# Two more ScalarE functions (ln, exp) in place of a VectorE add and reciprocal, in the sigmoid of a small condition vector

## The chip, the cores and the metric

The kernel runs on one core of one Trainium2 chip. The metric is device time in microseconds (us), from runs of the whole program. Before the change the median was 267.67 us of three runs (267.42 to 267.75). Times inside a run are from its one profile, in us from the start of the span.

## The reference, cut to what matters

The program is one transformer block with an adaptive layer norm. A condition vector `c` of 512 numbers is turned into six vectors that scale, shift and gate the rest:

```python
mod = (_silu(c) @ w_mod).reshape(c.shape[0], 6, 1, -1)
sa, ca, ga, sb, cb, gb = (mod[:, 0].copy(), mod[:, 1].copy(), ...)   # cut
h = _layernorm(x, axis=-1) * (1 + ca) + sa
x = x + ga * _A_ref(h, A_wqkv, A_wo)        # attention, window of 256
h = _layernorm(x, axis=-1) * (1 + cb) + sb
x = x + gb * _B_ref(h, B_w1, B_b1, B_w2, B_b2)   # MLP over the tokens
```

`x` is 2048 x 512, `w_mod` 512 x 3072. `silu(c) = c * sigmoid(c)` is 512 numbers, and all that follows needs it.

## The kernel before

The condition lies as a tile `c4` of 4 partitions by 128. Its sigmoid is exp on ScalarE, then add and reciprocal on VectorE. TensorE transposes silu (`st`), and two groups of 16 small matmuls (`fm`, tile `ps_fm`) multiply it with two slices of `w_mod`, which give the shift `sa` and the scale `ca`. Further names in the profiles: `mv` is the mean and variance of a tile of x, `nm` and `rs` are made from it (minus the mean, one over the root of the variance), `xn` is the normalised x, `sT` the copy of the transposed silu, `pxy` also the target of the warm-up matmuls, `lz` and `et` are the logarithm and the exponentials of the attention.

```python
o1 = op("em", {"ACT": 0.23}, lambda e: ac.activation(out=em[:], in_=c4[:], func=ACT.Exp, scale=-1.0), deps=[o_c4], pos=-20)
o2 = op("em1", {"DVE": 0.13}, lambda e: ve.tensor_scalar_add(out=em[:], in0=em[:], scalar1=1.0), deps=[o1], pos=-20)
o3 = op("rm", {"DVE": 0.9}, lambda e: ve.reciprocal(out=rm[:], in_=em[:]), deps=[o2], pos=-20)
o4 = op("silu", {"DVE": 0.2}, lambda e: ve.tensor_tensor(out=silu4[:], in0=c4[:], in1=rm[:], op=ALU.mult), deps=[o3], pos=-20)
o5 = op("st", {"PE": 0.03}, e_stps, deps=[o4], pos=-20, cls="D", alloc="psd")
```

Two further parts matter. First, TensorE starts with warm-up matmuls on a tile of zeros, whose result nobody reads; there are 24, and 14 of them stand in front of `st` in TensorE's order:

```python
warm_ops = [op("warm", {"PE": 0.213}, e_warm, pos=-30.0 + n * 0.3, cls="D") for n in range(WARM)]
```

Second, the order of instructions on every engine is fixed by a list of numbers (`ORDER`), so the program keeps a later instruction of an engine behind one that waits. On VectorE the add and the reciprocal stand between the statistics of the first and the second tile of x, and silu stands behind the latter. The table of functions for exp and ln is loaded once, at the start: `nc.scalar.preload_act_table_set("natural_log_exp_and_others")`.

The softmax here doesn't subtract the row's maximum and nothing guards it: scores larger than these inputs give would overflow.

## Time and profile before

| What | Before |
|---|---|
| span of the profiled run | 265.2 us |
| TensorE, VectorE, ScalarE busy | 248.8, 195.5, 185.4 us |
| the add and the reciprocal on VectorE | 0.21 and 0.94 us |
| silu ready | 6.58 us |
| last of the 14 warm-ups starts | 6.61 us |
| transposition `st` starts | 6.92 us |
| second slice of `w_mod` landed | 7.24 us |
| both groups of `ps_fm` ended | 8.41 us |
| first large exponential of the attention (`et`) starts | 17.73 us |

### The profile page before, as it was taken

What the parts mean: (1) busy time and instruction counts of PE and PEld (TensorE: products, weight loads), DVE (VectorE), ACT (ScalarE), POOL (GpSimd) and SP (SyncE); (2) the same over time, 40 slices, a digit from 0 to 9 for tenths busy, and PEclk for the clock granted to TensorE, in tenths of its full rate; (3) what the DMA queues carried; (4) which work ended last, traced back from release to release, by engine and by line L of the source; (5) the groups of instructions that cost most, each with busy time, mean ns of one, the idle gap of its engine ahead of it and who ended that gap; (6) DMA issues with size and microseconds to landing.
All of it is one profiled execution on the core that took longest, in us unless ns stands there. A gap on an engine that the chain in (4) does not pass through costs nothing.

```text
span 265.2 us, 10676 instructions
## 1 busy us (share of the span) xinstructions
PE 248.8 (94%) x4769; PEld 136.8 (52%) x4769; DVE 195.5 (74%) x444; ACT 185.4 (70%) x268; POOL 91.1 (34%) x153
## 2 busy tenths in 40 slices
PE   7898999999989888899999999999999999999993
PEld 2575666656656654455544454445444444444441
DVE  7768896777847559999948888999998730415875
ACT  2479999999999899999999999999416432000000
POOL 8054321495289946543893031440000000000000
PEclk9999999999999999999999999999999999999999
DMA  6996400000018000000015872011499800001122
GB/s 205 362 381 206 47 5 4 5 2 5 2 31 213 5 4 5 0 5 2 4 27 136 220 184 79 5 44 40 143 373 397 355 4 0 20 0 63 59 99 79
DMA packets 31598, 25.34 MB, mean 96 GB/s; under 512 B 6076, under 2 KB 29632, under 8 KB 31552
## 3 DMA queue, kind: packets, MB, share of 16 engines
q1 hardware_dynamic: 31544, 24.66, 29.5%
q8 instruction: 37, 0.61, 0.9%
q14 instruction: 9, 0.07, 0.1%
q10 hardware_dynamic: 8, 0.00, 0.0%
HBM read 22.55 MB, written 2.10 MB: 93 GB/s over the span
## 4 chain that ended last, share of the span: by engine, by line
PE 67%; ACT 19%; DVE 8%; issue 4%; POOL 0%; ACTq 0%; POOLq 0%
PE pu L194 32%; ACT et L194 16%; PE pxy L194 13%; PE psa L194 8%; PE pq L194 5%; PE pa L194 4%; PE pv L194 3%; ACT lz L194 3%; DVE st L194 2%; DVE VT L194 1%; PE pt L194 1%; DVE part L194 1%; PE psb L194 1%; DVE h L194 1%; DVE mv L194 0%
## 5 line engine op out<-in xcount | busy, mean ns | idle before, releaser
L194 ACT ACTIVATE et<-psa 128x1536 bf16<-128x1536 f32 x75 | 109.2, 1455 | 4.0 <-PE psa L194 1.9
L194 PE MATMUL pu<-hb,w1p 128*128 128x512 bf16 x224 | 53.2, 380 | 0.7 <-DVE part L194 0.7
L194 PE MATMUL pu<-guT,w 128*128 128x512 bf16 x224 | 49.0, 379 | 0.0
L194 ACT ACTIVATE et<-psb 128x512 bf16<-128x512 f32 x75 | 45.1, 601 | 0.0
L194 PE MATMUL pxy<-et,ones_bd 128*32 128x192 bf16 (+3 forms) x960 | 38.7, 233 | 0.7 <-issue 0.7
L194 PE MATMUL pxy<-et,VT 128*32 128x192 bf16 (+3 forms) x960 | 38.4, 234 | 0.9 <-DVE OT L194 0.5
L194 PEld LDWEIGHTS <-w 128*128 128x128 bf16 x224 | 21.9, 98 | 26.4
L194 PE MATMUL psa<-QT,KT 32*128 32x192 bf16 (+3 forms) x720 | 30.0, 230 | 5.6 <-ACT et L194 4.9
L194 POOL TENSOR_SCALAR KT<-kb,mask_par 128x512 bf16<-128x512 bf16 (+1 forms) x36 | 22.9, 645 | 31.0 <-DVE kb L194 22.3
L194 PEld LDWEIGHTS <-w1p 128*128 128x128 bf16 x224 | 20.2, 98 | 25.6 <-issue 2.3
L194 PE MATMUL pq<-h1T,wqkv 128*128 128x512 bf16 (+1 forms) x128 | 30.1, 355 | 0.3 <-ACT VT L194 0.3
L194 PEld LDWEIGHTS <-KT 32*128 32x128 bf16 x960 | 16.2, 92 | 26.4 <-issue 24.1
L194 PEld LDWEIGHTS <-VT 128*32 128x32 bf16 x960 | 23.6, 96 | 11.6 <-issue 10.1
L194 PE MATMUL psb<-QT,KT 32*128 32x192 bf16 (+3 forms) x240 | 29.4, 231 | 0.0
L194 DVE SCALAR_TENSOR_TENSOR o<-pu,b2FM,bc_all 128x512 f32<-128x512 f32 x16 | 11.6, 748 | 20.2 <-PE pu L194 20.1
L194 DVE TENSOR_TENSOR et<-et,maskt 128x512 bf16<-128x512 bf16 (+2 forms) x56 | 24.9, 480 | 0.6 <-ACT et L194 0.5
L194 PEld LDWEIGHTS <-ones_bd 128*32 128x32 bf16 x960 | 23.2, 97 | 1.0 <-issue 0.9
L194 DVE BATCH_NORM_STATS2 st<-x 128x6 f32<-128x512 bf16 x32 | 21.8, 680 | 0.2
L194 DVE TENSOR_TENSOR OT<-pxy,lz 128x256 bf16<-128x256 f32 x32 | 13.4, 419 | 10.6 <-ACT lz L194 10.1
L194 PEld LDWEIGHTS <-wqkv 128*128 128x128 bf16 x192 | 14.0, 97 | 13.4 <-issue 4.8
L194 PE MATMUL pv<-wqkv,h1T 128*32 128x256 bf16 x512 | 17.9, 274 | 0.2 <-DVE VT L194 0.2
L194 PE MATMUL pa<-wod,OT 128*128 128x512 bf16 x64 | 17.3, 381 | 0.3 <-ACT part L194 0.3
(113 smaller groups left out, 355.1 us busy)
## 6 DMA issues: line engine op xcount, KB each, us to landing
w1p<-in_B_w_dram SPq DMA_DIRECT2D x14, 512.0 KB, 6.3
w<-in_B_w_dram SPq DMA_DIRECT2D x14, 512.0 KB, 8.3
wmod<-in_w_mod_dram SPq DMA_DIRECT2D x6, 512.0 KB, 5.5
x<-in_A_x_dram SPq DMA_DIRECT2D x16, 128.0 KB, 4.6
out_dram<-otile SPq DMA_DIRECT2D x16, 128.0 KB, 1.7
wqkv<-in_A_wqkv_dram SPq DMA_DIRECT2D x2, 384.0 KB, 5.5
wqkv<-in_A_wqkv_dram SPq DMA_DIRECT2D x1, 512.0 KB, 5.3
wod<-in_A_wo_dram SPq DMA_DIRECT2D x1, 512.0 KB, 8.7
```

The costliest lines, as they stand in the source:

```text
L194: ins = call(*args, **kwargs)
```

## The change

The intent is to take the slow reciprocal off VectorE: 1/(1+y) is computed as exp(-ln(1+y)), all on ScalarE, which idles there.

```diff
-    o2 = op("em1", {"DVE": 0.13}, lambda e: ve.tensor_scalar_add(out=em[:], in0=em[:], scalar1=1.0), deps=[o1], pos=-20)
-    o3 = op("rm", {"DVE": 0.9}, lambda e: ve.reciprocal(out=rm[:], in_=em[:]), deps=[o2], pos=-20)
+    o2 = op("em1", {"ACT": 0.25}, lambda e: ac.activation(out=rm[:], in_=em[:], func=ACT.Ln, bias=1.0), deps=[o1], pos=-20)
+    o3 = op("rm", {"ACT": 0.25}, lambda e: ac.activation(out=rm[:], in_=rm[:], func=ACT.Exp, scale=-1.0), deps=[o2], pos=-20)
```

In the built program VectorE has two instructions fewer and ScalarE two more. TensorE, GpSimd and the DMA queue have the same instructions in the same order.

## The prediction

> **What bounds the kernel now.** I read the page first, for which engine carries the span, then the chain that ended last in order of time over the first 30 us, because the changed operations run once, near the start. The first line below is the busy time of the engines, the second the share of the chain by engine.
>
> ```profile
> PE 248.8 (94%) x4769; PEld 136.8 (52%) x4769; DVE 195.5 (74%) x444; ACT 185.4 (70%) x268; POOL 91.1 (34%) x153
> ...
> PE 67%; ACT 19%; DVE 8%; issue 4%; POOL 0%; ACTq 0%; POOLq 0%
> ```
>
> TensorE is busy nearly throughout and carries two thirds of the chain. VectorE is busy for 74% of the span but carries 8% of the chain, so a microsecond of VectorE is by default not a microsecond of kernel. The question is whether this particular microsecond is one of the 8%. The chain around it (start, duration, what):
>
> ```profile
> 1.33 5.66 PE pxy L194 x14
> 6.99 0.10 PE st_ps L194
> 7.09 0.54 PE pxy L194 x2
> 7.63 0.78 PE ps_fm L194 x32
> 8.41 0.47 PE psb L194 x8
> ```
>
> The reader is to see that from 1.33 us to 6.99 us the chain lies on fourteen matmuls into pxy. They are the warm-up matmuls on a zeroed tile, whose results nobody reads. Right behind them comes st_ps, the transposition of silu(c), which is the only consumer of what the change touches. No link of the sigmoid (em, rm, silu) is in the chain. Next the timeline of VectorE alone from 4.2 us to the end of its row of work (start, duration, operation):
>
> ```profile
> 4.36 0.18 DVE L194 BATCH_NORM_AGGREGATE mv<-st 128x2 f32<-128x6 f32 x1
> 4.46 0.21 DVE L194 TENSOR_SCALAR em<-em 4x128 f32<-4x128 f32 x1
> 4.70 0.94 DVE L194 RECIPROCAL rm<-em 4x128 f32<-4x128 f32 x1
> 5.57 0.62 DVE L194 BATCH_NORM_STATS2 st<-x 128x6 f32<-128x512 bf16 x1
> 6.23 0.18 DVE L194 BATCH_NORM_AGGREGATE mv<-st 128x2 f32<-128x6 f32 x1
> 6.33 0.25 DVE L194 TENSOR_TENSOR silu<-c,rm 4x128 bf16<-4x128 bf16 x1
> 6.51 0.14 DVE L194 SCALAR_TENSOR_TENSOR nm<-mv 128x2 f32<-128x2 f32 x1
> ```
>
> VectorE has no idle time here: the statistics of the second x tile wait behind the reciprocal, silu waits behind those, and silu is ready at 6.33 + 0.25 = 6.58 us. ScalarE in the same stretch:
>
> ```profile
> 0.79 1.28 ACT L204 ACT_TABLE_LOAD   x1 [0.79 <-PEq L1251]
> 2.17 0.31 ACT L194 ACTIVATE em<-c 4x128 f32<-4x128 bf16 x1
> 6.45 0.30 ACT L194 ACTIVATE rs<-mv,eps_t 128x2 f32<-128x2 f32 x1 [3.97 <-DVE mv L194]
> 6.78 0.20 ACT L194 ACTIVATE rs<-rs 128x2 f32<-128x2 f32 x1
> ```
>
> It idles 3.97 us between em and rs, which is exactly where the two new functions go. Last, the handover itself, from the timeline of all engines:
>
> ```profile
> 6.92 0.09 PEld L194 LDWEIGHTS <-silu 4*128 4x128 bf16 x1 [0.42 <-DVE nm L194]
> 6.92 0.17 PE L194 MATMUL st_ps<-identity,silu 4*128 4x4 bf16 x1
> ...
> 7.13 0.16 DVE L194 COPY sT<-st_ps 128x4 bf16<-128x4 bf16 x1 [0.48 <-PE st_ps L194]
> ```
>
> The bracket says that the weight load of silu sat 0.42 us and was released by VectorE. So the deadline is nearly a tie: silu is ready at 6.58 us, and TensorE comes to it at about 6.8 us. I take that number from the last warm-up matmul, which I saw start at 6.61 us; at the fast cadence of 0.22 us it hands over at 6.83 us. The transposition started at 6.92 us, about 0.09 us later than that.
>
> **What the Trainium skill says.** "ScalarE: Activation LUTs", section "What ACT_TABLE_LOAD costs", gives an ACTIVATE with immediate scale and bias 186 ns + 0.833 N, and about 93 ns more for a pointer operand. For N = 128 that is 293 ns; the trace has 0.31 us for em. The pointer term agrees too: rs with the eps_t bias takes 0.30 us, rs without it 0.20 us, on the same shape. The same page, section "Table sets: the hidden batching unit", says that natural_log_exp_and_others holds both exp and ln. The kernel loads that set at its start (the one load of 1.28 us above) and already runs ln and exp for rs back to back with no load between 6.45 and 6.98 us, so the trace agrees. "TensorE: Matmul & The Clock Gate", Part 1, says that the first matmuls run with a start-to-start of 426.7 ns at N = 512 and later ones at 215.7 ns, and that the moment of the change depends on a free-running window and so varies between runs. Here the warm-ups step at about 0.43 us from the first on and only the last step, 6.39 to 6.61 us, is 0.22 us, so the cadences agree; that the moment varies is not shown by one trace.
>
> **The change part by part.** *Removed from VectorE:* the add (0.21 us) and the reciprocal (0.94 us). What counts is not their sum but how far the row behind them can move up: the second statistics start at 5.57 us and could start where the add started, 4.46 us, which is 1.11 us. Nothing else holds them, as the second x tile was issued at 1.2 us and landed 2.1 us later, about 3.35 us. So mv is done at about 5.30 us, silu at 5.47 us and nm at 5.54 us. The order of VectorE's other instructions is unchanged in the built program, as are all of TensorE's, GpSimd's and the DMA queue's.
>
> *Added to ScalarE:* ln of 4x128 with a bias: 0.31 (row em) plus at most 0.09-0.10 (rs with a bias against rs without) = 0.40 us; exp of 4x128: 0.31 us. With two handovers of 0.03 us (rs to rs: 6.75 to 6.78 us), rm is ready at 2.48 + 0.03 + 0.40 + 0.03 + 0.31 = 3.25 us. Silu cannot run before about 5.2 us because the statistics stand in front of it, so ScalarE has almost 2 us in hand. The 0.71 us of new ScalarE work costs nothing: it lies in the idle 3.97 us. rs follows mv at about 5.3 us.
>
> *Moved:* silu 6.58 to 5.47 us. Its consumer cannot start before the fourteen warm-ups are through, about 6.83 us, so of the 1.11 us only the tie of 0.09 us is collected at st_ps. There may be another 0.1 us right after it: with silu ready early its weight load can lie under the last warm-up instead of in front of the transposition (the next warm-up started at 7.03 us, 0.11 us after st_ps). That makes 0.1 to 0.2 us on the chain at ps_fm. The second group of ps_fm needs the second wmod slice, landed at about 2.2 + 5.1 = 7.3 us and used at about 7.85 us, so the transfer leaves room for it. The row of xn on VectorE stands behind sT in program order, so having rs 1.1 us earlier buys nothing by itself. From there to the end nothing changes but this offset; some of it can be lost again wherever a transfer sets the pace. Sum: -1.11 us on VectorE, +0.71 us on an idle ScalarE, about -0.15 us on the chain. 267.67 - 0.15 = 267.5 us.
>
> **The rivals.** First, *the reciprocal is on the path and the whole microsecond comes back*: 267.67 - 1.1 = 266.6 us. For it speaks the bracket on silu's weight load and the full VectorE row. Against it: the chain names the warm-ups up to 6.99 us, and the warm-ups keep their place before the transposition. It could come true in part if the clock opens earlier in the timed runs; were it four matmuls earlier, the warm-ups would end 4 x 0.21 = 0.8 us sooner and the old kernel, not the new one, would wait. The second wmod slice at 7.3 us then caps the gain at about 0.6 us: 267.1 us.
>
> Second, *ScalarE becomes the late one*: a table switch hidden in ln or exp, twice 1.28 us, would put rm at 3.25 + 2.56 = 5.8 us and silu at about 6.1 us, still ahead of 6.83 us; rs would be held slightly. Even this gives about 267.7 us. Against it: the set is loaded, and the built program has only the two new rows on ScalarE.
>
> Third, *the offset is swallowed or turned round later*: the main stretch alternates TensorE and ScalarE, and shifting the start by 0.1 us against transfers already under way could change a meeting of VectorE with GpSimd or of a buffer with its load. I give this a few tenths of a microsecond either way: 267.2 to 268.0 us.
>
> **Range and chances.** The three runs before spread 0.33 us. All mechanisms above end between 266.6 and 268.0 us; the expected one is 267.5 us. I choose 266.9 to 268.1 us: the cap of the first rival less some scatter below, the third rival plus scatter above. Two per cent is 5.35 us, nearly five times all the VectorE work removed and more than any rival can produce, so "within 2%" is close to certain.
>
> **What would show it right or wrong.** In the changed profile VectorE should have the second statistics at about 4.46 us and silu done by 5.5 us; ScalarE two new rows of 0.3 to 0.4 us before 3.4 us and no second table load before the gelu part; rs at about 5.3 us. The weight load of silu should no longer wait for VectorE, st_ps should start between 6.8 and 6.95 us, and the chain should still show fourteen warm-ups in front of it. VectorE should show a longer idle gap before sT, from 0.48 us to about 1.5 us: the microsecond freed turned into waiting. I am wrong if st_ps moves by more than 0.5 us with the warm-ups stepping as now, if rm is ready after 5.2 us, or if a later stretch moves by more than half a microsecond with the start unchanged.

## The result, and the profile after

The changed kernel takes 267.51 us (median of 4 runs, 266.67 to 267.74), the kernel before 267.71 us (4 runs, 267.42 to 268.0). The ratio is 0.9987, with a 95% interval of 0.9963 to 1.0011: no difference. Ratios here are the mean time of one kernel's runs over that of the other's of the same rounds, so not quite the ratio of the medians quoted. The page of the changed kernel, engines and chain:

```profile
PE 243.6 (92%) x4727; PEld 136.7 (51%) x4769; DVE 194.9 (73%) x442; ACT 186.1 (70%) x270; POOL 90.7 (34%) x153
...
PE 62%; ACT 20%; DVE 9%; issue 5%; DMA 2%; POOL 0%; SPq 0%; ACTq 0%; POOLq 0%
```

VectorE lost 0.6 us net and ScalarE gained 0.7 us, of a span of 266.0 us. (42 of TensorE's 4769 matmul records are missing from this trace, which is why its busy time looks smaller.) New in the chain is DMA with 2%. The timeline of all engines between 0.7 and 10 us shows the moved work (start, duration, engine, operation):

```profile
2.52 0.31 ACT L194 ACTIVATE rm<-em 4x128 f32<-4x128 f32 x1
2.86 0.31 ACT L194 ACTIVATE rm<-rm 4x128 f32<-4x128 f32 x1
...
4.46 0.66 DVE L194 BATCH_NORM_STATS2 st<-x 128x6 f32<-128x512 bf16 x1
...
5.26 0.26 DVE L194 TENSOR_TENSOR silu<-c,rm 4x128 bf16<-4x128 bf16 x1
...
6.11 0.09 PEld L194 LDWEIGHTS <-silu 4*128 4x128 bf16 x1 [0.42 <-issue]
...
6.32 0.16 DVE L194 COPY sT<-st_ps 128x4 bf16<-128x4 bf16 x1 [0.73 <-PE st_ps L194]
...
7.61 0.55 PE L194 MATMUL ps_fm<-sT,wmod 128*128 128x1 bf16 x16 [0.41 <-DMA wmod<-in_w_mod_dram]
```

ScalarE has rm at 3.17 us, two microseconds before anyone asks for it. VectorE's row moved up from 5.57 to 4.46 us, the 1.11 us of the prediction, and silu is ready at 5.52 us, 1.06 us earlier. Then two things are to be seen. The weight load of silu still sat 0.42 us, the same figure as before, although silu had now been ready for 0.59 us: the bracket named VectorE before and names nothing now ("issue"), so those 0.42 us were never a wait for silu. And the second group of ps_fm, which ran through without a gap before, now waits 0.41 us for a transfer. The chain says the same (start, duration, what):

```profile
2.16 5.40 DMA wmod<-in_w_mod_dram
7.56 0.05 issue
7.61 0.55 PE ps_fm L194 x16
```

Here the transposition came 0.81 us earlier than in the first profile (6.11 against 6.92 us), the end of ps_fm 0.25 us earlier (8.16 against 8.41 us), and the first et 0.25 us earlier (17.48 against 17.73 us). But the 0.81 us are more than silu's row can explain: TensorE itself was through with the fourteen warm-ups 0.81 us earlier (last start 5.80 against 6.61 us). Eight of their steps were slow (about 0.43 us) in this execution and twelve before; later steps take 0.22 us, and four steps at 0.21 us less make the 0.81 us. The trace's own records of the granted TensorE clock begin where the steps turn short: at 4.70 us here, at 6.36 us before. TensorE's order is the same in both programs, so one execution of each does not tell the change from the clock. Nor does the end: between the 41st and the last of the 75 large et this profile took 74.82 us and the one before 74.28 us, half a microsecond lost near 138 us, where nothing of the change is left. As much again was lost behind the last et, so that this span is 0.8 us longer although its first et came earlier.

### The profile page after: what moved, and what is told of

It reads as the page before. It is cut to its first block, busy times and chain, and to the rows that moved or that the text cites. A ratio compares the mean times of both kernels' runs of the same rounds, so it can differ in the third digit from the quotient of the medians.

```text
span 266.0 us, 10635 instructions
## 1 busy us (share of the span) xinstructions
PE 243.6 (92%) x4727; PEld 136.7 (51%) x4769; DVE 194.9 (73%) x442; ACT 186.1 (70%) x270; POOL 90.7 (34%) x153
## 4 chain that ended last, share of the span: by engine, by line
PE 62%; ACT 20%; DVE 9%; issue 5%; DMA 2%; POOL 0%; SPq 0%; ACTq 0%; POOLq 0%
PE pu L194 32%; ACT et L194 16%; PE pxy L194 10%; PE psa L194 7%; PE pq L194 5%; PE pv L194 3%; ACT lz L194 3%; PE pa L194 3%; DMA wmod<-in_w_mod_dram 2%; DVE st L194 2%; DVE h1T L194 1%; DVE part L194 1%; DVE VT L194 1%; DVE et L194 1%; DVE OT L194 1%
## 5 line engine op out<-in xcount | busy, mean ns | idle before, releaser
L194 PE MATMUL pu<-hb,w1p 128*128 128x512 bf16 x212 | 51.5, 380 | 2.2 <-DVE st L194 1.3
L194 PE MATMUL pq<-h1T,wqkv 128*128 128x512 bf16 (+1 forms) x112 | 27.4, 351 | 1.3 <-issue 0.8
L194 DVE TENSOR_TENSOR et<-et,maskt 128x512 bf16<-128x512 bf16 (+2 forms) x56 | 25.6, 491 | 0.6 <-ACT et L194 0.5
L194 PE MATMUL pa<-wod,OT 128*128 128x512 bf16 x56 | 15.9, 381 | 1.4 <-issue 0.5
```

The costliest lines, as they stand in the source:

```text
L194: ins = call(*args, **kwargs)
```

## The experiments

Theory W says that the warm-ups, and behind them the second slice of `w_mod`, hold TensorE, so that VectorE's freed microsecond turns into waiting. Theory R says that the reciprocal set the start and its time comes back. Twelve kernels were run, all correct in their results. First the milestones from all profiles but that of sigmoid_alone, then each run. "Slow steps" counts the steps over 0.3 us between starts of the warm-ups in front of `st`; the expectations say 10 for the first profile, because two steps of just 0.40 us were not counted there.

| Kernel | slow steps | silu ready | `st` starts | 2nd slice landed | ps_fm ends | first et |
|---|---|---|---|---|---|---|
| before | 12 of 13 | 6.58 | 6.92 | 7.24 | 8.41 | 17.73 |
| before_again | 13 of 13 | 6.57 | 7.24 | 7.38 | 8.73 | 18.05 |
| changed kernel | 8 of 13 | 5.52 | 6.11 | 7.56 | 8.16 | 17.48 |
| after_again | 13 of 13 | 5.52 | 7.26 | 7.79 | 8.75 | 18.08 |
| after_refilled | 13 of 13 | 6.59 | 7.31 | 7.12 | 8.80 | 18.12 |
| sigmoid_reload | 9 of 13 | 5.52 | 6.35 | 7.95 | 8.55 | 17.87 |
| before_recip1 | 9 of 13 | 7.39 | 7.45 | 7.06 | 8.94 | 18.26 |
| before_recip4 | 12 of 13 | 10.31 | 10.37 | 6.89 | 12.35 | 22.30 |
| before_8warm | 7 of 7 | 6.59 | 6.65 | 7.23 | 8.14 | 17.51 |
| after_8warm | 7 of 7 | 5.52 | 5.58 | 7.99 | 8.59 | 18.49 |
| after_two_moved | 9 of 13 | 5.53 | 6.24 | 7.40 | 8.00 | 17.07 |
| after_new_order | 9 of 9 | 5.52 | 5.71 | 7.89 | 8.55 | 17.61 |
| before_new_order | 8 of 9 | 6.59 | 6.65 | 7.48 | 9.64 | 19.31 |

### before_again and after_again: both kernels once more, unchanged

No edit.

> The kernel before, unchanged, as a null control. Theory W (the fourteen warm-up matmuls in front of the transposition of silu hold it; the change collects only the lag of silu behind them): ratio 1.000 within 0.002. The number of slow steps (about 0.43 us) among the warm-ups may differ from the 10 of the first profile; silu stays ready at about 6.58 us whatever it is, and st_ps starts at the later of silu + 0.1 us and the end of the warm-ups, so 6.7 to 7.4 us. Theory R (the reciprocal sets the start): st_ps stays within 0.1 us of 6.92 us however the warm-ups step. First large exponential (et) at 17.7 us, within 0.3 us. If the loss of about half a microsecond near 138 us in the changed kernel's profile belongs to that execution and not to the change, this profile may show such a step too.

> The changed kernel, unchanged, timed in five rounds. Theory W: ratio 0.998 to 1.000 (0 to 0.5 us faster). silu ready at about 5.5 us; st_ps at the end of the warm-ups: about 6.1 us with 8 slow steps, about 6.8 us with 10 or 11. The second half of ps_fm not before the second wmod slice lands (7.2 to 7.6 us). First et at 17.4 to 17.6 us against 17.73 us before. Theory R: 1.1 us faster (ratio 0.996), first et at about 16.6 us.

before_again took 267.49 us (4 runs), ratio 1.0009 (0.9993 to 1.0025). after_again took 267.22 us (6 runs), ratio 1.0001 (0.9989 to 1.0013). Both stand against the same 11 runs of the kernel before, median 267.15 us. The two profiles happen to be a matched pair: all thirteen steps are slow, and the clock records begin at 7.00 and 7.05 us. The handover in before_again, from the timeline of all engines:

```profile
7.24 0.09 PEld L194 LDWEIGHTS <-silu 4*128 4x128 bf16 x1 [0.66 <-DVE nm L194]
7.24 0.17 PE L194 MATMUL st_ps<-identity,silu 4*128 4x4 bf16 x1
...
7.45 0.16 DVE L194 COPY sT<-st_ps 128x4 bf16<-128x4 bf16 x1 [0.80 <-PE st_ps L194]
```

The same in after_again:

```profile
7.26 0.09 PEld L194 LDWEIGHTS <-silu 4*128 4x128 bf16 x1 [0.68 <-issue]
7.26 0.17 PE L194 MATMUL st_ps<-identity,silu 4*128 4x4 bf16 x1
...
7.47 0.16 DVE L194 COPY sT<-st_ps 128x4 bf16<-128x4 bf16 x1 [1.89 <-PE st_ps L194]
```

silu was ready 1.06 us earlier in after_again, and the transposition started at the same time, within 0.02 us; so did the first et (18.08 against 18.05 us). The freed time stands in VectorE's bracket in front of sT: 0.80 us of idling became 1.89 us. The chain of after_again still has the fourteen warm-ups in front of `st` (start, duration, what):

```profile
1.33 6.00 PE pxy L194 x14
7.33 0.11 PE st_ps L194
```

With equal warm-ups, late as these are, the change is worth nothing at the start, as W says, and R's 1.1 us are not there. W's expectations of silu, `st` and the ratios held. Those of the first et did not: 18.05 us is just over the 17.7 us within 0.3 us that I gave for before_again, and 18.08 us outside the 17.4 to 17.6 us for after_again, because I had assumed a clock that opens as early as in the first profiles. The loss near 138 us is absent here (74.28 us from the 41st to the last et, 74.29 us in before_again), so it belonged to one execution.

### after_refilled: the old VectorE work put back beside the new ScalarE work

```diff
+        ac.activation(out=rm[:], in_=em[:], func=ACT.Ln, bias=1.0)
+        ve.tensor_scalar_add(out=scr[:], in0=em[:], scalar1=1.0)
...
+        ac.activation(out=rm[:], in_=rm[:], func=ACT.Exp, scale=-1.0)
+        ve.reciprocal(out=scr[:], in_=scr[:])
```

> The changed kernel, with the old add and reciprocal put back into the same place of VectorE's order, but writing to a tile that nobody reads. It tells the VectorE slot from the ScalarE route. If the slot alone made the shift (both W and R say so): VectorE's second statistics back at about 5.57 us, silu at 6.58 us, st_ps at 6.7 to 6.95 us unless the warm-ups end later, first et at 17.7 us, ratio 1.000 within 0.002. A third theory, that silu being fed from ScalarE matters by itself (wait on another engine), would leave silu elsewhere than 6.33 to 6.58 us.

267.23 us, ratio 1.0004 (0.9988 to 1.0019). The second statistics are back at 5.57 us and silu at 6.33 to 6.59 us, as in the kernel before, although rm was ready at 3.17 us. So it was the slot in VectorE's row that moved silu, and nothing about where rm comes from. `st` followed the warm-ups (all thirteen steps slow) at 7.31 us.

### before_recip1 and before_recip4: more reciprocals in the old place

```diff
+        ve.reciprocal(out=rm[:], in_=em[:])
+        for _ in range(1):          # 4 in before_recip4
+            ve.reciprocal(out=scr[:], in_=em[:])
```

> The kernel before with one more reciprocal of 4x128 behind the first one (result unused): VectorE's row moves 0.85 to 0.95 us later, silu ready at about 7.5 us. Theory W has a knee: before the change silu is already the later of the two by 0.1 to 0.6 us, so every further microsecond counts in full: st_ps at about 7.6 us, the first et at 18.2 to 18.6 us, total +0.5 to +0.9 us, ratio 1.002 to 1.003. Theory R says the same of this direction (+0.9 us). A theory that the start does not matter for the end (later stretches absorb it) says ratio 1.000.

> The kernel before with four more reciprocals of 4x128 (results unused): silu ready about 3.6 us later, at about 10.2 us. If a delay at the start comes through to the end undiminished: st_ps at about 10.3 us, first et near 21 us, total +3.2 to +3.6 us, ratio 1.012 to 1.0135. If later stretches swallow delays: ratio under 1.006. This gives the slope on the late side, against which the slope on the early side (the change: 1.11 us taken out) is compared: W says about 0.2 of the 1.11 us come back, R says all.

before_recip1: 267.79 us against 267.15 us, ratio 1.0023 (1.0010 to 1.0036). silu is 0.82 us later, at 7.39 us, and now `st` follows it within 0.06 us: this is what a TensorE that waits for silu looks like. First et at 18.26 us, total +0.6 us, as expected of W. But I had placed the knee wrongly: silu was not "already the later of the two" before. With a lag of 0.06 us `st` could have started at about 6.63 us in the two profiles of the kernel before; it started 0.29 and 0.61 us later, and so of the 0.82 us only 0.53 us are seen against the first of them (7.45 against 6.92 us).

before_recip4: 271.84 us against 267.04 us, ratio 1.0182 (1.0162 to 1.0202), where I had expected at most 1.0135. silu came when expected (10.31 us) and `st` at 10.37 us, 3.45 us late; but the first et is 4.57 us late. The windows of this kernel tell why (us, then busy time of TensorE, weight loads, VectorE, ScalarE, GpSimd, then the granted TensorE clock, DMA share and GB/s):

```profile
6.00:8.00 2.00, 0.96 (x4) 0.25 (x2) 1.93 (x3) 0.00 (x0) 0.64 (x1) 1.00 1.16 329
8.00:10.00 2.00, 0.00 (x0) 0.00 (x0) 1.93 (x4) 0.00 (x0) 0.00 (x0) 0.93 1.07 359
10.00:12.00 2.00, 1.63 (x28) 1.07 (x28) 1.32 (x7) 0.50 (x2) 0.00 (x0) 0.50 1.10 374
12.00:14.00 2.00, 1.78 (x31) 1.53 (x29) 0.65 (x5) 1.16 (x3) 0.00 (x0) 0.50 1.09 380
```

TensorE idled from 6.96 to 10.37 us, and from about 9.7 us its clock was halved for 6.8 us. So a late silu costs its lateness and, if TensorE runs dry meanwhile, a second fee. The curve has a knee: behind it every VectorE microsecond counts in full or more (from one to four extra reciprocals silu came 2.92 us later, the first et 4.04 us), in front of it none does, and the kernel before stood in front of it in both of its profiles.

### before_8warm and after_8warm: six of the fourteen warm-ups left out

```diff
+        box["warms"] = box.get("warms", 0) + 1
+        if 9 <= box["warms"] <= 14:
+            return
```

> The kernel before with six of the fourteen warm-ups in front of st_ps left out (the results of warm-ups are not read). Theory W: the eight warm-ups end at about 4.8 us even if all step slowly, so silu alone holds st_ps, at about 6.65 to 6.75 us; gain at most 0.2 us against before unless the TensorE clock opens later for lack of work. Theory R: st_ps at 6.9 us as before. First et 17.4 to 18.0 us; ratio 0.998 to 1.002.

> The changed kernel with the same six warm-ups left out: now neither the warm-ups nor VectorE's reciprocal stand before st_ps. Both theories: st_ps follows silu at about 5.55 to 5.65 us, 1.1 us earlier than in the kernel before with eight warm-ups. Theory W adds that the next bound takes over at once: the second wmod slice, landing at 7.2 to 7.6 us, so that ps_fm still ends at 8.0 to 8.2 us and the first et starts at 17.3 to 17.6 us (ratio 0.998 to 1.000). If nothing else were in the way, the first et would start near 16.6 us (ratio 0.996).

With the warm-ups out of the way silu alone holds `st`: 6.65 us in before_8warm, 5.58 us in after_8warm, 1.07 us apart. (The bracket of `st` in before_8warm names GpSimd's memset of VT, which happens to end at 6.65 us as well; it ended there in after_8warm too, where `st` had started at 5.58 us, so `st` does not wait for it.) That is theory R's microsecond, and the next bound takes it: in after_8warm the two groups of ps_fm waited 0.40 and 0.79 us for the two slices of `w_mod` (the second landed at 7.99 us in that execution), and ps_fm ended at 8.59 us, later than the 8.14 us of before_8warm and than the 8.0 to 8.2 us expected. That the slice takes over is what W said; the first et missed its 17.3 to 17.6 us by 0.9 us. The times did not come out as expected: 268.74 us, ratio 1.0078 (1.0049 to 1.0107), and 268.61 us, ratio 1.0072 (1.0035 to 1.0109). The windows of before_8warm, columns as above:

```profile
4.00:6.00 2.00, 0.93 (x3) 0.02 (x1) 1.93 (x5) 0.00 (x0) 2.00 (x6) 1.00 1.05 368
...
8.00:10.00 2.00, 1.95 (x25) 1.12 (x23) 1.25 (x6) 1.49 (x4) 0.00 (x0) 0.66 1.09 379
10.00:12.00 2.00, 2.00 (x8) 1.03 (x7) 1.93 (x9) 1.45 (x4) 0.00 (x0) 0.50 1.10 376
```

TensorE idled 1.72 us (4.93 to 6.65 us), and the clock fell to half between 8.65 and 12.06 us; in after_8warm, with idle stretches of 0.65, 0.40 and 0.79 us, it fell as well. So the warm-ups that hide the change also keep the clock up. But the lost clock is not what made before_8warm slow: its first et came at 17.51 us, 0.22 us earlier than in the first profile of the kernel before (from the end of ps_fm to the first et it took 9.37 us, and 9.90 us in after_8warm, against 9.32 us at full clock). It lost its time later, at full clock: 0.36 us between the fifth and the sixth large et and 1.02 us in front of the 65th, where its chain has TensorE standing with no wait that the profile shows (start, duration, what):

```profile
29.85 0.62 issue
...
158.37 0.76 issue
```

after_8warm lost 0.24 and 0.76 us at the same places. Of the kernels with all 24 warm-ups only sigmoid_alone, with its table loads, loses time there, and no run settles the cause. The profiled run of before_8warm is the fastest of its four (267.70 us), so the profile does not show all that the others lost.

### sigmoid_reload and sigmoid_alone: one Sigmoid function, with and without calling the table set back

```diff
+        ac.activation(out=rm[:], in_=c4[:], func=ACT.Sigmoid)     # for exp, ln and exp
+        ac.preload_act_table_set("natural_log_exp_and_others")    # not in sigmoid_alone
```

> The changed kernel with one Sigmoid function on ScalarE in place of exp, ln and exp, and two switches of the function table around it (two more table loads of 1.28 us each). It is the rival of a late ScalarE, made on purpose: rm ready at about 3.7 us, the second load through at about 5.0 us, before rs is wanted at 5.38 us. Theory W: no cost; silu at 5.3 to 5.5 us, st_ps and the first et as in the changed kernel, ratio 0.998 to 1.000. If ScalarE's start were critical: +1.0 to +2.6 us (ratio 1.004 to 1.010).

> The changed kernel with one Sigmoid function and nothing that calls the joint exp-and-ln set back: the built program then chooses a set for each function by itself and has 87 table loads in place of 2 in the program of the changed kernel. At 1.28 us each, 85 more loads are 109 us of ScalarE work, and ScalarE carries the attention part: 300 to 375 us in all. It shows why the change uses three functions of one set, and that ScalarE time in the main stretch counts where the 0.6 us at the start did not.

sigmoid_reload: 267.04 us, against 267.04 us for before in the same rounds, ratio 1.0010 (0.9984 to 1.0035), a hair above the 0.998 to 1.000 expected and not told from it. Its first et at 17.87 us is later than the changed kernel's because its second slice landed late, at 7.95 us. Timeline of ScalarE:

```profile
2.08 1.28 ACT L194 ACT_TABLE_LOAD   x1
3.37 0.31 ACT L194 ACTIVATE rm<-c 4x128 f32<-4x128 bf16 x1
3.69 1.28 ACT L194 ACT_TABLE_LOAD   x1
5.38 0.29 ACT L194 ACTIVATE rs<-mv,eps_t 128x2 f32<-128x2 f32 x1 [0.41 <-DVE mv L194]
```

Even two table loads, 2.56 us of extra ScalarE work, fit in front of rs, which still starts at 5.38 us as in the changed kernel. The rival of a late ScalarE is refuted with 0.41 us to spare.

sigmoid_alone: 377.41 us (one run, state unknown; I had said 300 to 375). Groups of instructions of this kernel, costliest first (busy us, mean ns):

```profile
L194 ACT ACT_TABLE_LOAD x86 | 110.3, 1283 | 3.4 <-DVE a L194 1.9
```

Once the joint set is no longer the active one, the built program changes tables between ln and exp all through the attention, and with 110 us of loads the total rose by 110 us. That the two agree so well is partly chance, as the granted clock of that run was 0.90 in the mean, against 1.00 in the runs of the kernel before. Still, the same 1.28 us cost nothing in ScalarE's hole at the start and about full price in the stretch that ScalarE carries.

### after_two_moved: work moved into the freed hole

Only the order list is edited: the reduction for `mask_par` moves right behind nm, the copy `sT_rep` behind sa, both out of VectorE's full row behind 9 us.

```diff
 VectorE's order
   nm
+  mask_par
   sT, xn, xn, modFM, sa, sa
+  sT_rep
   modFM, qkb, qkb, st, mv
-  mask_par
   h1T, st, mv, KT, KT
-  sT_rep
   QT
```

> The changed kernel with two VectorE instructions taken out of the busy row behind 9 us and put into the hole in front of and behind sT: the reduction that makes mask_par (0.31 us for the pair, needs nothing but the identity) right behind nm, and the copy sT_rep (0.22 us) behind sa. In the chain of the kernel before they held 0.23 and 0.15 us. Theory W, in its general form (freed time of an engine that is off the chain is worth what is moved into it): the KT products on VectorE and all behind them come 0.3 to 0.4 us earlier for the same end of ps_fm; the first large et starts 8.9 to 9.1 us after ps_fm ends, against 9.32 us in all four profiles so far of kernels with the old order; ratio 0.998 to 1.000. If VectorE's row there is not what holds the start: no change in that distance.

266.96 us against 267.26 us, ratio 0.9995 (0.9973 to 1.0017). From the end of ps_fm to the first et it takes 9.07 us (8.00 to 17.07), and 9.32 us in all seven profiles above with the old order and the full clock. So 0.25 us are gained there, as expected; the timing cannot resolve a tenth of a per cent. The chain of the changed kernel shows this row of VectorE: between 9.06 and 12 us it lies on qkb, st, mv, mask_par, h1T, so there the time counts.

### after_new_order and before_new_order: TensorE's order adapted to an early silu

Both have the two moves, and this order on TensorE (two warm-ups are left out):

```diff
 TensorE's order
-  14 warm-ups, st, 2 warm-ups, 16 ps_fm, 16 ps_fm, 8 transpositions of xn
+  10 warm-ups, st, 2 warm-ups, 16 ps_fm, 8 transpositions of xn, 2 warm-ups, 16 ps_fm
```

> The changed kernel with the same two moves and TensorE's order adapted to the early silu: ten warm-ups in front of st_ps, not fourteen; behind it two warm-ups, the first half of ps_fm, the eight transpositions of xn, two more warm-ups, then the second half of ps_fm; two warm-ups left out. TensorE should not fall idle for over half a microsecond before 8 us, so its clock should stay granted. Theory W: st_ps at about 5.6 to 5.75 us (silu ready at 5.5 us), the second half of ps_fm as soon as its wmod slice lands (7.0 to 8.0 us), h1T right behind it; first et at 16.4 to 17.2 us, ratio 0.996 to 0.999. If the clock is lost as with six warm-ups left out: granted clock 0.5 somewhere between 8 and 12 us, ratio over 1.002.

> The kernel before (add and reciprocal on VectorE) in exactly the order of the kernel after_new_order. It shows what the change itself is worth once TensorE's order no longer hides it. Theory W: silu ready at about 6.6 us holds st_ps at 6.65 us, TensorE idles for about a microsecond in front of it; the first half of ps_fm at about 7.2 us, the second at about 8.2 us; first et 0.3 to 0.7 us later than in after_new_order, more if the idle microsecond costs the clock. Ratio 0.998 to 1.006 to before. If the change is worth nothing in any order: the same first et within 0.1 us (allowing for when the wmod slices land).

Neither beats the kernel before: 268.14 us, ratio 1.0031 (1.0011 to 1.0051), and 269.18 us, ratio 1.0071 (1.0050 to 1.0091), against 267.26 us. Against each other they show about what the change is worth in an order that needs it: the mean of the six runs is 268.09 us with the change and 269.15 us without, 1.06 us less (one of the six runs with it is above the lowest without). `st` came 0.94 us and the end of ps_fm 1.09 us earlier with it, the first et 1.71 us, where I had expected 0.3 to 0.7 us. Part of that is the clock: before_new_order idled 1.27 us in front of `st` and then ran at half the clock from 8.24 to 15.07 us, after_new_order kept the clock. Its first et at 17.61 us missed my 16.4 to 17.2 us, because the slices landed late in that execution (6.54 and 7.89 us) and ps_fm ended at 8.55 us. And it lost 0.9 us more between the fifth and the sixth large et, and 1.0 us in front of the 65th; before_new_order lost 0.65 us at the first place and under 0.1 us at the second. So the difference of the totals also holds pauses that have nothing to do with silu. The chain of after_new_order (start, duration, what) has at the first place:

```profile
29.65 1.24 issue
```

TensorE stood 1.24 us and waited for nothing that the profile shows; before_new_order stood 0.97 us at the same place. All four kernels with warm-ups left out have this pause; the others do not. I have no run that settles the cause.

## Why the prediction was right or wrong

The total was right: 267.5 us predicted, 267.51 us measured, ratios of 0.9987 and 1.0001 in two sets of rounds. That the last digit fits is chance, as the runs of one kernel spread over a microsecond.

*What bounds the start.* Right for the kernel before, and for the changed kernel where the clock opens late. In the matched pair TensorE went from the warm-ups to `st` at 7.24 and 7.26 us whether silu was ready at 6.57 or 5.52 us. Where it opened early (the first profile of the changed kernel), the second slice of `w_mod` was the bound, and "the transfer leaves room for it" did not hold: it landed at 7.56 us and ps_fm waited 0.41 us.

*What is removed from VectorE.* Right: 1.11 us for the row, silu at 5.52 us where 5.47 was predicted. after_refilled shows that it is the slot.

*What is added to ScalarE.* Right in place, a little high in size: ln took 0.31 us where the sum had 0.40. The constant bias of 1.0 did not cost what the eps_t bias costs (0.30 against 0.20 us). The formula of the Trainium skill that the prediction quotes ("ScalarE: Activation LUTs", section "What ACT_TABLE_LOAD costs") comes within 0.02 us of this ln and of both rs, if 1.0 counts as an immediate.

*The tie of 0.09 us, and another 0.1 us behind it.* This step failed. I read "[0.42 <-DVE nm]" together with a start 0.09 us behind the cadence as a short wait for silu. In the changed kernel silu is early, and `st` still starts 0.31 us behind the last warm-up (5.80 to 6.11), exactly as before (6.61 to 6.92), and the next warm-up still comes 0.11 us behind `st`. So the lag does not come from silu: there was no wait to collect, and none of it was collected. The term of the sum should have been 0, not 0.15 us; the gain at ps_fm in the matched pair was 0 (8.73 and 8.75 us).

*The first rival.* It had the better picture of the changed kernel's first profile: the clock opened four slow steps earlier, just the case that it named, and VectorE's old row, which never let `st` start before 6.65 us in any profile, would then have held it. The cap I gave it was real too: the second slice of `w_mod` took over at 7.56 us. ps_fm ended at 8.16 us there; before_8warm, with the old VectorE row and its slice at 7.23 us, ended it at 8.14 us. So even with an early clock little or nothing remains, unless the slice comes early too. An estimate from the clock and the slice of each of the ten profiles with all fourteen warm-ups (`st` at 6.63 us or behind the warm-ups, whichever is later, for the old row; ps_fm ends 1.49 us behind `st`, or 0.60 us behind the slice) gives a gain of 0.35 us for those of before_recip1, of 0.10 and 0.12 us for sigmoid_alone and after_two_moved, and 0 for the other seven: 0.06 us in the mean, which the timing cannot tell from nothing. It is not shown, as no profile caught the kernel before with an early clock and all its warm-ups.

*The second rival* is refuted by sigmoid_reload. *The third*, shifts later on, was real in size, half a microsecond near 138 us and another behind the last et in one execution, but is not put down to the change: the repeat does not have it.

*The signs.* VectorE's and ScalarE's rows came as forecast; VectorE's gap in front of sT was 0.73 and 1.89 us, where about 1.5 us were forecast. `st` did not fall between 6.8 and 6.95 us in either profile of the changed kernel (6.11 and 7.26 us), and the chain of the first has the slice's transfer where the fourteen warm-ups were forecast; the move of 0.81 us is no sign against the mechanism, because the warm-ups did not step as before.

*The chances.* "Within 2%", called close to certain, was right, and the reason given holds: only with four more reciprocals and a lost clock did the start move the total by 1.8%.

## What to carry to other kernels

Removing work from an engine pays only up to the point where its consumer next has a free hand; find that point before counting the saving, and look for the bound behind it as well. A bracket that names a releaser shows what came last, not that it was late: compare with an execution in which it came early. Work placed in front of a consumer only to keep a clock up can hide an improvement, and taking it away can cost more than the improvement is worth; here a part of that cost came as pauses 20 us and more later, so look at the whole span before naming the cause.

## What the Trainium skill lacked or had wrong

- "TensorE: Matmul & The Clock Gate", Part 1, says that the number of slow matmuls at the start varies between runs. The runs agree: 8 to 13 slow steps of 13 among kernels with the same fourteen warm-ups. It says not to fit a model to one such count, but not what follows for comparing two profiles: the start of `st` moved by 1.15 us from that alone (6.11 and 7.26 us for the same kernel).
- The same page, section "Why this matters for your kernels", names idle gaps of TensorE over about 3 us as those to avoid lest the clock fall. Here 1.72 us (before_8warm) and 1.27 us (before_new_order) were each followed by half the clock, and so were three gaps of 0.65, 0.40 and 0.79 us within 3.1 us (after_8warm), while one of 1.10 us (before_recip1) was not. One profile each.
- "VectorE: DVE Perf Modes" tells how the reciprocal is computed but not what it costs. On 4x128 in f32 it took 0.94 us, against 0.21 us for an add of a constant on the same shape; four in a row took 3.81 us.
- No page warns that the granted clock of the windows can read 1.00 in the first microseconds while matmuls of 512 columns still step at 0.43 us, as in all profiles here. That 1.00 is no measurement: the trace's clock records begin only when the steps turn short (at 4.70 us in the changed kernel, at 6.36 us before), and time without a record is counted as full clock.
- No page that I read tells how to settle the cause of a pause of TensorE like the 1.24 us at 29.65 us in after_new_order, in which the profile shows no wait.
